# Three edits to a planned single-core kernel: who issues 32 stores, when four weight conversions run, and how far apart four weight combinations lie

## The chip, the cores and the metric

The program runs on 1 core of one Trainium2 chip. The metric is the device time of one execution in microseconds (us); less is better. Before the change it was 1371.14 us, the median of three runs (1365.4 to 1371.9).

The engines by their names in the rows: PE is the matrix engine (PEld its weight load), DVE the vector engine, ACT the scalar engine, POOL is GpSimd, and SP is the sync engine, which here only issues transfers (DMAs). A DMA stands in the instruction stream of the engine that issues it (SP, POOL or ACT); it can be issued only when all earlier instructions of that engine have been issued, and the data land some us later.

## The reference, cut to what matters

```python
# attention in chunks of 64 rows over q, k, v of shape (8, 8, 576, 64)
scores = matmul(q_c, k_c.T) / sqrt(64);  attn = softmax(scores);  out = matmul(attn, v_c)
x = out.transpose(0, 2, 1, 3).reshape(4608, 512)
# first MLP: 512 -> 2048 -> 512, softplus between
h = x @ w_in;  g = maximum(h, 0) + log1p(exp(-abs(h)));  x = g @ w_out
# second MLP: 512 -> 768 (three products, maximum of them) -> 512
y = maximum(maximum(x @ w1, x @ w2), x @ w3) @ w_out2
```

## The kernel before

**Numbers.** Products are wanted in near fp32. Every operand is kept as a high and a low part (`cut_up`: a copy to the rounded format gives the high part, a subtraction the low), and a product is three matmuls (high*high, high*low, low*high). The weights come as 64-bit floats; `conv` (lines 297 to 364) loads them as pairs of 32-bit words and builds the value on DVE in six steps (L332, L339, L346, L351, L357, L360), of which the last gives a rest that is added or cut up after it.

**Tiling.** The 4608 rows are nine blocks of 512. Each block has 16 steps of the first MLP (`mlp1`): an inner product (L805) into `ph`, softplus on ACT, `cut_up` into a buffer `g`, and an outer product (L825) into two accumulators `acc`.

**Stages in time.** (1) Blocks 0 to 2 (the blocks of `NP = 3`) go through `mlp1` step by step, in turns: block 0 steps 0 to 3, block 1 steps 0 to 7, block 0 steps 4 to 15, block 1 steps 8 to 15, block 2 steps 0 to 15. Meanwhile DVE converts the weights of the first MLP, and attention tiles for later blocks run (`attention`: loads of q, k and v, transposes on DVE, scores into `aps`, softmax, the probabilities `p` out to a DRAM buffer `pd` and back in another layout, values). (2) The other six blocks go in three pairs. A pair (A, B) has eight units (`UnitA`): seven products of half size (L1120, a Strassen scheme, products p1 to p7) give softplus inputs for two steps of both blocks. Softplus values of A (`h == 0`) are cut up into `g` at once and used by `mlp1_out` (L1419); those of B (`h == 1`) are written to DRAM (`gd`, line 1162, 16 in each of the first two pairs) and read again (line 1400) when A is done and B's 16 outer products follow. The third pair goes another way (`Sevens`): it keeps B's values on the chip and takes quarter products with combinations of the outer weights, which `combos` makes beforehand (16 DRAM tiles `wso`). (3) The second MLP (`Triple`) takes combinations of w1, w2 and w3 (`weights3`, DRAM tiles `w2c`), made from weights that `early` converted in stage 1 or 2 and stored (`w2d`, line 869; `wo2d`).

**What sets the order.** The kernel records operations with costs, inputs and due times, and `Plan.order` lays them out: a list scheduler with a modelled clock starts what is ready, the most urgent first, on an engine that is idle in its model, and gives out buffers. The result is a fixed order on every engine. So a change to a cost, an engine or a table shifts orders, buffers and waits of many operations near it. DMAs on SP and ACT take one of eight completion semaphores in turn (`DMAHW0` to `DMAHW7` in the rows of the built program; POOL's are `DMASW0` to `7`), and each waits, before it is issued, for the DMA that had the semaphore before it.

**Places touched.** `EARLIES` (line 978) says how many conversions `early` adds at each unit of each pair; `COMBOS` (line 986) after which of block B's outer products `combos` starts; line 1162 in `UnitA.soft` issues the store of a softplus value of B.

Of the kernel before, what the change touches and what calls it, by code (L numbers as in the profile page):

```python
# [183 lines left out]
def tile_kernel(ctx: ExitStack, tc: tile.TileContext, q, k, v, w_in, w_out, w1, w2, w3, wo2, out):  # L184
    nc = tc.nc
    B, H, S, D = q.shape
# [7 lines left out]
    NJ2 = DH2 // P  # L194
# [59 lines left out]
    gd = [[dram.tile([P, TB], F32, name=f"gd{i}_{j}") for j in range(NJ)] for i in range(3)]  # L254
# [36 lines left out]
    T0, STEP = 30.0, 6.0  # L291
# [674 lines left out]
    clock = [T1]  # L966
# [8 lines left out]
    EARLY = 8  # L975
    GATE = 7
    SPLITS = 6
    EARLIES = ((0, 0, 1, 1, 1, 1, 1, 1), (1,) * 8, (2, 2, 1, 1, 1, 1, 1, 1))
    GROUPS = (0, 1, 2, 3, 4, 6, 7)
    LATE_GROUPS = (1,)  # L980
    SPLIT = 1
# [1 line left out]
    GDLAT = 8.0  # L983
    SOON = 4
    SEVENS = (2,)
    COMBOS = (('out', 0, 1), ('out', 0, 4), ('out', 0, 7), ('out', 0, 10))
    LATER = (7, 0)
    SLACK = 0.0
    MORE = (3, 0), (5, 0), (5, 0)
# [113 lines left out]
    class UnitA:  # L1103
# [39 lines left out]
        def soft(u, src, z, fh):  # L1143
            c, (f, h) = u.c[fh], fh
            j = 2 * u.n + f
            if u.q in SEVENS:
                z2, at = raw_of(u.q, u.n, f, h), u.n % 2
                y = lambda: z2.t[:, at]
                in_line("y", op(
                    {"A": 0.62}, lambda e: nc.scalar.activation(y(), src(), AF.Softplus), r=[z], w=[(z2, at)], alloc=first_of(z2)  # L1150
                ))
                if h == 0:
                    g = second["a", NP + 2 * u.q, j] = Buf("g")
                    cut_up(g, y, [(z2, at)], alloc=[g])
                return
            in_line("y", op({"A": 0.62}, lambda e: nc.scalar.activation(c.t, src(), AF.Softplus), r=[z], w=[c], alloc=[] if z is c else [c]))
            if h == 0:
                g = second["a", NP + 2 * u.q, j] = Buf("g")
                cut_up(g, lambda: c.t, [c], alloc=[g])
            else:  # L1160
                store["g", u.q, j] = op(
                    {"S": 0.48}, lambda e: nc.sync.dma_start(out=gd[u.q][j], in_=c.t), r=[c], lat=6.0, move=1.1
                )

        def p1(u):
# [532 lines left out]

    def strassen():

        outs, earlies = [], 0
        tile_at = HP * NP + 2 * HP + 2

        def out(n=1):
# [14 lines left out]
        for q in range(pairs):  # L1719
            A, B = NP + 2 * q, NP + 2 * q + 1  # L1720
# [6 lines left out]
            for n, m in enumerate(ORDER[q]):  # L1727
                clock[0] = T0 + STEP * NJ * A + 17.7 * n
                new = UnitA(q, m)
                begin = new.p1()  # L1730
                mark["unit", q, n] = begin
                if ("unit", q, n) in COMBOS:
                    combos(COMBOS.index(("unit", q, n)), [begin], clock[0] + 30.0)
                if n == SEVENS_LOAD and sevens:
                    mark["sevens", q] = begin
                for _ in range(EARLIES[q][n]):
                    early(earlies, clock[0] + STEP * EARLY, [begin])
                    earlies += 1
                if q == pairs - 1:
                    mark[n] = begin  # L1740
                if not sevens:
                    out()
                if old:
                    old.p5()
                    old.p4()
                    if sevens:
                        out()
                    later(old.n, 1)
                new.p6()
                if old:  # L1750
                    old.p3()
                else:
                    out()
                new.p2()
                if not old:
                    out()
                new.p7()
                if n in GROUPS:
                    group()
                out()  # L1760
                later(m, 0)
                old = new
# [16 lines left out]
            for j in range(NJ - 2):  # L1779
                o = out()  # L1780
                if ("out", q, j) in COMBOS:
                    combos(COMBOS.index(("out", q, j)), [o], clock[0] + 30.0)
# [14 lines left out]
        for q in range(NB // 3):  # L1797
            u = Triple(q, banks, gate)
# [6 lines left out]
            for p in todo:  # L1805
# [3 lines left out]
                begin = u.product(*p, alloc=both if both[0].first is None else [])  # L1809
# [15 lines left out]
    for n, f in enumerate((1.0, -1.0)):  # L1825
        op(
            {"D": 0.2},
            lambda e, n=n, f=f: nc.vector.tensor_scalar(eye.t[:, n, :P], ident, f, None, ALU.mult),
# [8 lines left out]
    for j in range(NJ):  # L1837
# [4 lines left out]
        for t in range(HP, 2 * HP) if j == 1 else ():  # L1842
            attention_first(t, [line["load"]])
    tiles = 2 * HP
    for n, (b, j, first, last) in enumerate(steps):
        if n >= NJ and n % (NJ // HP) == 0:
            t = HP + n // (NJ // HP)
            t = 2 * HP + (n - NJ) // 2
            while tiles <= t + 1 and tiles < 22:
                attention(tiles, [first_loads[tiles if tiles < 2 * HP + 3 else NJ - 1]])  # L1850
                tiles += 1
        h = mlp1(b, j, first, last)
        if ("step", b, j) in COMBOS:
            combos(COMBOS.index(("step", b, j)), [h], T0 + STEP * (n + 4))
        if b == NP - 1 and j % 2 == 0:
            weightsa(j // 2, [before_last], lead)
        if (b, j) == (1, NJ // 2):
            lead = h
        before_last = h if j % 2 == 0 else before_last
# [38 lines left out]
```

## Time and profile before

| | |
|---|---|
| median of three runs | 1371.14 us (1365.4, 1371.14, 1371.9) |
| the profiled execution's own time | 1365.48 us |
| span of the profile, first to last instruction | 1363.6 us |
| PE busy | 1333.2 us, 98% of the span |
| DVE, ACT, POOL busy | 983.7, 545.0, 321.7 us |
| mean granted PE clock | 0.994 |

The span and 1.9 us around it make the execution's time. Busy time is a sum over stages; a stage is read by its own rows: in which stretch PE stands idle, on whom it waits there, and what that one waits for. "Idle before" names the engine or DMA whose end released an instruction; "issue" means that nothing in the profile explains the time (for an engine that issues DMAs, mostly a completion semaphore of an earlier DMA).

### The profile page before, as it was taken

The page shows a single profiled execution, that of the slowest core. Times are in us where ns is not written, and L with a number is a line of the kernel's source. Part 1 is how long each engine was busy: PE and PEld are TensorE (multiplying, and loading weights), DVE is VectorE, ACT ScalarE, POOL GpSimd, SP SyncE. Part 2 cuts the span into 40 slices and gives each one's busy share as a digit, 9 for nine tenths or more (in the row PEclk, how much of TensorE's full clock was granted, in tenths as well). Part 3 has the DMA queues.
Part 4 walks back from the last instruction along what each step waited for, and adds up shares of the span by engine and source line. Part 5 has one row for each costly group of instructions (what it writes and reads, how often), then busy time and mean ns, then how long its engine had stood idle before and what let it go on. Part 6 is the DMA issues. An engine that isn't in the chain of part 4 may idle for free.

```text
span 1363.6 us, 23089 instructions
## 1 busy us (share of the span) xinstructions
PE 1333.2 (98%) x8616; PEld 1094.0 (80%) x8616; DVE 983.7 (72%) x1527; ACT 545.0 (40%) x1199; POOL 321.7 (24%) x561
## 2 busy tenths in 40 slices
PE   5899999999999999999999999999999999999998
PEld 4788887888888887787788887888888888888887
DVE  8999965797576898657868898779714597145951
ACT  4544434464544645445535454432123222132211
POOL 2011555542233324323211122121111122011100
PEclk8999999999999999999999999999999999999999
DMA  8565567677689999978966789655644465344401
GB/s 254 159 201 154 134 181 201 189 273 228 169 257 258 267 302 301 280 252 297 366 209 237 259 311 338 234 192 193 219 162 144 155 231 206 141 148 154 139 25 68
DMA packets 218863, 289.38 MB, mean 212 GB/s; under 512 B 121601, under 2 KB 146625, under 8 KB 218753
## 3 DMA queue, kind: packets, MB, share of 16 engines
q0 software_dynamic: 53792, 178.26, 38.1%
q1 hardware_dynamic: 164144, 108.87, 26.9%
q8 instruction: 68, 1.11, 0.3%
q10 hardware_dynamic: 816, 0.79, 0.2%
q14 instruction: 43, 0.34, 0.1%
HBM read 196.61 MB, written 91.23 MB: 211 GB/s over the span
## 4 chain that ended last, share of the span: by engine, by line
PE 86%; DVE 5%; issue 4%; DMA 2%; POOL 1%; ACT 1%; SPq 0%; DVEq 0%; POOLq 0%; ACTq 0%
PE acc L1567 14%; PE both L1567 13%; PE acc L825 10%; PE ph L805 9%; PE ph L1120 8%; PE acc L1419 7%; PE one L1120 6%; PE both L1665 6%; PE acc L1665 5%; PE acc L1342 2%; PE ph L1342 2%; PE acc L1265 2%; DVE s L288 1%; PE aps L503 1%; POOL rv L468 1%
## 5 line engine op out<-in xcount | busy, mean ns | idle before, releaser
L288 DVE TENSOR_TENSOR s<-s,s 128x1024 f32<-128x1024 f32 (+3 forms) x222 | 213.8, 992 | 11.8 <-DMA x2d<-s 5.5
L1419 PE MATMUL acc<-g,s 128*128 128x512 f32 x768 | 184.5, 393 | 3.0 <-ACT tmp L281 2.2
L1419 PEld LDWEIGHTS acc<-g,s 128*128 128x128 f32 x768 | 142.6, 188 | 35.2 <-ACT tmp L281 3.1
L1120 PE MATMUL ph<-s,s 128*128 128x512 f32 x576 | 144.1, 389 | 1.4 <-DMA s<-wac 0.7
L805 PE MATMUL ph<-s,s 128*128 128x512 f32 x576 | 140.4, 394 | 0.0
L825 PE MATMUL acc<-g,s 128*128 128x512 f32 x576 | 139.8, 392 | 0.0
L1120 PEld LDWEIGHTS ph<-s,s 128*128 128x128 f32 x576 | 108.0, 188 | 24.6 <-DMA s<-wac 1.2
L805 PEld LDWEIGHTS ph<-s,s 128*128 128x128 f32 x576 | 108.3, 189 | 23.1
L825 PEld LDWEIGHTS acc<-g,s 128*128 128x128 f32 x576 | 107.3, 188 | 22.6
L281 ACT CAST s<-s 128x512 fp32r<-128x512 f32 (+1 forms) x106 | 86.3, 831 | 93.4 <-DVE s L1598 31.2
L1567 PE MATMUL acc<-s,s 128*128 128x512 f32 x452 | 120.3, 389 | 0.0
L1550 POOL DMA_DIRECT2D s<-w2c x105 | 56.0, 533 | 266.2 <-PE both L1567 87.5
L281 ACT CAST g<-s 128x1024 fp32r<-128x1024 f32 (+1 forms) x64 | 58.7, 919 | 144.6 <-PE both L1567 37.3
L1567 PE MATMUL acc<-g,s 128*128 128x512 f32 x400 | 110.0, 389 | 0.0
L1120 PE MATMUL one<-s,s 128*128 128x512 f32 x432 | 106.4, 390 | 0.9 <-ACT p L562 0.9
L1567 PE MATMUL both<-s,s 128*128 128x512 f32 x400 | 106.3, 389 | 0.0
L288 DVE TENSOR_TENSOR g<-tmp,g 128x512 fp32r<-128x512 f32 x104 | 70.6, 680 | 44.3 <-ACT g L281 44.2
L1567 PE MATMUL both<-g,s 128*128 128x512 f32 x368 | 100.1, 389 | 0.0
L1567 PEld LDWEIGHTS acc<-s,s 128*128 128x128 f32 x452 | 84.9, 188 | 17.6
L1120 PEld LDWEIGHTS one<-s,s 128*128 128x128 f32 x432 | 80.9, 188 | 18.5 <-ACT p L562 1.8
L468 POOL DMA_DIRECT2D rv<-in_v_dram x103 | 63.5, 620 | 104.5 <-issue 55.3
L1567 PEld LDWEIGHTS both<-s,s 128*128 128x128 f32 x400 | 75.1, 188 | 15.6
(158 smaller groups left out, 2159.5 us busy)
## 6 DMA issues: line engine op xcount, KB each, us to landing
s<-w2c POOLq DMA_DIRECT2D x105, 512.0 KB, 4.5
s<-wac POOLq DMA_DIRECT2D x66, 512.0 KB, 6.5
w2c<-s POOLq DMA_DIRECT2D x45, 512.0 KB, 5.2
wac<-s POOLq DMA_DIRECT2D x24, 512.0 KB, 5.1
s<-in_moe_w_dram POOLq DMA_DIRECT2D x18, 512.0 KB, 5.6
s<-x2d POOLq DMA_DIRECT2D x18, 512.0 KB, 5.8
s<-in_moe_w_in_dram SPq DMA_DIRECT2D x16, 512.0 KB, 6.2
s<-in_moe_w_out_dram SPq DMA_DIRECT2D x16, 512.0 KB, 5.7
```

The costliest lines, as they stand in the source:

```text
L281: nc.scalar.copy(dst(), src())
L288: return op({"D": 0.69 * n}, lambda e: nc.vector.tensor_tensor(dst(), a(), b(), f), r=r, w=w, **kw)
L468: dma(out=dst().rearrange("p (c e d) -> p c e d", e=2, d=D)[half * CH:(half + 1) * CH, lo:lo + mine, h, :], in_=v[b, t % HP * 2 + h].rearr ...
L805: nc.tensor.matmul(ph.t, w[:, wi, kk * P:(kk + 1) * P], x[kk].t[:, xi], start=(kk == 0 and wi == 0 and xi == 0), stop=(kk == KD - 1 and wi ...
L825: nc.tensor.matmul(acc[m // 2].t[:, m % 2], w[:, wi, m * P:(m + 1) * P], g.t[:, gi, :], start=(first and wi == 0 and gi == 0), stop=(last ...
L1120: nc.tensor.matmul(dst(), ws.t[:, wi, col + kk * P:col + (kk + 1) * P], x[kk].t[:, xi], start=(first and kk == 0 and wi == 0 and xi == 0), ...
L1265: nc.tensor.matmul(u.acc[f].t[:, m], w.t[:, wi, m * P:(m + 1) * P], g.t[:, gi, :], start=(first and wi == 0 and gi == 0), stop=(last and w ...
L1342: nc.tensor.matmul(dst(m), lhs(wi, nn, m), (GH, GL)[gi].t[:, nn], start=(fresh and nn == 0 and wi == 0 and gi == 0), stop=(nn == 1 and wi ...
L1419: nc.tensor.matmul(acc[half].t[:, m % 2], w.t[:, wi, m * P:(m + 1) * P], g.t[:, gi, :], start=(first and wi == 0 and gi == 0), stop=(last ...
L1550: lambda e, k=k, z=z: nc.gpsimd.dma_start(out=z.t.bitcast(F32), in_=w2c[s][late + k]),
L1567: nc.tensor.matmul(bank.view()[:, f], ws(wi, slice(f * HT + kk * P, f * HT + (kk + 1) * P)), (XH, XL)[xi].t[:, kk], start=(first and kk == ...
L1665: nc.tensor.matmul(banks[t // 2].view()[:, t % 2], (GH, GL)[gi].t[:, f, t * P:(t + 1) * P], wo2_of[j].t[:, wi], start=(j == 0 and wi == 0 ...
```

## The change

`BEFORE` is new: four conversions for the second MLP are recorded right after steps 9, 11, 13 and 15 of block 1 of the first MLP. They are the first four of the list; so the units of the first pair take six less two, none at its last two units, and the second pair takes none at its first two units. The total stays 24. `COMBOS` starts the four combinations after outer products 1, 5, 9 and 13 of block B of the first pair; before, after 1, 4, 7 and 10. The stores to `gd` are planned on ACT, at a cost of 0.5 in the plan, and issued there.

```diff
-    EARLIES = ((0, 0, 1, 1, 1, 1, 1, 1), (1,) * 8, (2, 2, 1, 1, 1, 1, 1, 1))
+    EARLIES = ((0, 0, 1, 1, 1, 1, 0, 0), (0, 0, 1, 1, 1, 1, 1, 1), (2, 2, 1, 1, 1, 1, 1, 1))
+    BEFORE = ((1, 9), (1, 11), (1, 13), (1, 15))
...
-    COMBOS = (('out', 0, 1), ('out', 0, 4), ('out', 0, 7), ('out', 0, 10))
+    COMBOS = (('out', 0, 1), ('out', 0, 5), ('out', 0, 9), ('out', 0, 13))
...
                 store["g", u.q, j] = op(
-                    {"S": 0.48}, lambda e: nc.sync.dma_start(out=gd[u.q][j], in_=c.t), r=[c], lat=6.0, move=1.1
+                    {"A": 0.5}, lambda e: nc.scalar.dma_start(out=gd[u.q][j], in_=c.t), r=[c], lat=6.0, move=1.1
                 )
...
-        outs, earlies = [], 0
+        outs = []
...
                 for _ in range(EARLIES[q][n]):
-                    early(earlies, clock[0] + STEP * EARLY, [begin])
-                    earlies += 1
+                    early(next(earlies), clock[0] + STEP * EARLY, [begin])
...
+    earlies = iter(range(4 * NJ2 + 6))
     for n, (b, j, first, last) in enumerate(steps):
...
         h = mlp1(b, j, first, last)
+        if (b, j) in BEFORE:
+            early(next(earlies), T0 + STEP * (n + EARLY), [h])
```

The order on PE stays as it was but for one attention product, which moves behind one outer product. On the other engines it moves at many places. Three of them follow.

**ACT, first pair, where the values of steps 2 and 3 of block B are stored.** `tmp<-tmp` and `tmp<-ph` (L1156, in the new file L1157) are softplus; `CAST g<-tmp` gives the high part for an outer product; `COPY tmp<-ph` empties the bank into which PE's next product goes. Before:

```order
L1156 ACTIVATE tmp_79<-tmp_79 128x512 [waits DVE_49]
L1156 ACTIVATE tmp_83<-ph_93 128x512 [waits PE_49,Activation_49]
L281 CAST g_76<-tmp_83 128x512 [waits Activation_49]
L281 COPY tmp_85<-ph_92 128x512 [waits DMAHW1_49,PE_49]
L1156 ACTIVATE tmp_84<-tmp_84 128x512 [waits DVE_49]
L1156 ACTIVATE tmp_80<-tmp_80 128x512 [waits DVE_49]
L281 COPY tmp_86<-ph_92 128x512 [waits PE_49]
L281 CAST g_77<-tmp_80 128x512 [waits Activation_49]
```

Now:

```order
L1157 ACTIVATE tmp_84<-tmp_84 128x512 [waits DVE_49]
L1157 ACTIVATE tmp_85<-ph_93 128x512 [waits DMAHW0_49,PE_49]
L1163 DMA gd_3_110<-tmp_84 128x512 [waits DMAHW2_49,Activation_49]
L281 CAST g_76<-tmp_85 128x512 [waits Activation_49]
L281 COPY tmp_86<-ph_92 128x512 [waits DMAHW3_49,PE_49]
L1157 ACTIVATE tmp_82<-tmp_82 128x512 [waits DVE_49]
L1163 DMA gd_2_109<-tmp_82 128x512 [waits DMAHW0_49,Activation_49]
L1157 ACTIVATE tmp_83<-tmp_83 128x512 [waits DVE_49]
L281 COPY tmp_80<-ph_92 128x512 [waits DMAHW1_49,PE_49]
L281 CAST g_77<-tmp_83 128x512 [waits Activation_49]
```

Two stores stand in ACT's stream, one ahead of each copy out of `ph`; each waits for a completion semaphore that it shares with SP's DMAs, and for the softplus before it.

**DVE, second half of block 1 of the first MLP.** `mx` and `p` are an attention tile's softmax, L751 turns `p` for its way through `pd`, and L698 and L699 turn the next tile's q and k. Before:

```order
L288 TENSOR_TENSOR s_113_2790<-aps_94,s_113_2790 128x512
L698 STREAM_TRANSPOSE s_114_2811<-rq_74 128x512
L699 STREAM_TRANSPOSE s_114_2811<-tmp_78 128x512
L590 TENSOR_SCALAR mx_70<-mx_70 128x8
L591 RECIPROCAL mx_70<-mx_70 128x8
L288 TENSOR_TENSOR p_89<-p_89,mx_70 128x512
L751 STREAM_TRANSPOSE s_115_2853<-p_89 128x512
```

Now:

```order
L332 TENSOR_SCALAR tmp_86<-s_110_2638 128x512
L698 STREAM_TRANSPOSE s_114_2811<-rq_74 128x512
L339 TENSOR_SCALAR tmp_86<-tmp_86 128x512
L699 STREAM_TRANSPOSE s_114_2811<-tmp_78 128x512
L346 TENSOR_SCALAR tmp_86<-tmp_86 128x512
L351 SCALAR_TENSOR_TENSOR tmp_86<-s_110_2638,tmp_86 128x512
L590 TENSOR_SCALAR mx_70<-mx_70 128x8
L357 TENSOR_SCALAR tmp_79<-tmp_86 128x512
L591 RECIPROCAL mx_70<-mx_70 128x8
L360 SCALAR_TENSOR_TENSOR tmp_79<-s_110_2638,tmp_79 128x512
L288 TENSOR_TENSOR p_89<-p_89,mx_70 128x512
L288 TENSOR_TENSOR tmp_86<-tmp_86,tmp_79 128x512
```

A conversion's seven instructions lie between those of the softmax; its first, L332, waits for a weight load that POOL issues.

**POOL, from block B of the first pair into the second pair.** `wso` are the stores of the combinations, `wac` and `wae` loads of Strassen weights, `rv` an attention tile's values, and L318 the load that a conversion starts from. Before:

```order
L468 DMA rv_88<-in_v_dram 64x4x64 x2
L468 DMA rv_88<-in_v_dram 64x3x64 x2
L468 DMA rv_88<-in_v_dram 64x64 x2
L1233 DMA wso_3_231<-s_268_6096 128x1024
L318 DMA s_269_6135<-in_moe_w_dram 128x4x256
L1233 DMA wso_3_235<-s_270_6146 128x1024
L1045 DMA s_272_6183<-wac_2_163 128x1024
L1233 DMA wso_3_239<-s_271_6171 128x1024
L1233 DMA wso_3_243<-s_273_6187 128x1024
L1045 DMA s_275_6219<-wac_1_162 128x1024
L1045 DMA s_276_6257<-wae_180 128x1024
```

Now:

```order
L468 DMA rv_88<-in_v_dram 64x4x64 x2
L468 DMA rv_88<-in_v_dram 64x3x64 x2
L468 DMA rv_88<-in_v_dram 64x64 x2
L1234 DMA wso_3_231<-s_268_6094 128x1024
L1234 DMA wso_3_235<-s_270_6132 128x1024
L1234 DMA wso_3_239<-s_271_6160 128x1024
L1234 DMA wso_3_243<-s_272_6167 128x1024
L1046 DMA s_274_6199<-wac_2_163 128x1024
L1046 DMA s_275_6227<-wac_1_162 128x1024
L1046 DMA s_276_6264<-wae_180 128x1024
```

The load for a conversion is gone from here (as is one a little ahead of it), and the last four `wso` stores stand together, ahead of the Strassen loads.

## Rows read from the trace of the kernel before

**Rows 1.** The page: span and busy us by engine.

```profile
span 1363.6 us, 23089 instructions
PE 1333.2 (98%) x8616; PEld 1094.0 (80%) x8616; DVE 983.7 (72%) x1527; ACT 545.0 (40%) x1199; POOL 321.7 (24%) x561
```

**Rows 2.** Busy us by stretch: PE, PEld, DVE, ACT, POOL; clock, DMA share, GB/s.

```profile
0.00:40.00 40.00, 24.94 (x655) 19.82 (x656) 33.38 (x77) 17.48 (x50) 8.44 (x19) 0.84 0.85 251
...
200.00:345.00 145.00, 143.89 (x1222) 117.62 (x1216) 108.60 (x225) 75.30 (x267) 62.90 (x109) 1.00 0.74 223
345.00:440.00 95.00, 95.00 (x712) 77.96 (x711) 56.83 (x110) 45.17 (x135) 29.57 (x49) 1.00 0.81 236
440.00:560.00 120.00, 117.64 (x803) 94.61 (x802) 103.67 (x196) 63.81 (x183) 39.41 (x66) 1.00 0.96 291
...
600.00:720.00 120.00, 117.06 (x628) 95.31 (x628) 85.71 (x151) 59.47 (x118) 30.87 (x53) 1.00 0.80 285
```

**Rows 3.** PE's waits, 440 to 560 us: us, times, longest.

```profile
PE one L1120 <- ACT p L562: 0.9, 2, 0.6
PE ph L1120 <- DMA s<-wac: 0.7, 1, 0.7
PE acc L1419 <- DVE g L288: 0.4, 1, 0.4
PE acc L1419 <- ACT tmp L281: 0.3, 1, 0.3
```

**Rows 4.** PE's waits, 600 to 720 us.

```profile
PE acc L1419 <- ACT tmp L281: 2.0, 1, 2.0
PE ph L1120 <- ACT tmp L281: 0.7, 1, 0.7
PE acc L1419 <- DVE g L288: 0.3, 1, 0.3
```

**Rows 5.** PE's waits, 195 to 345 us.

```profile
PE aps L503 <- DMA s<-pd: 1.1, 2, 0.6
```

**Rows 6.** POOL in order of time, 536 to 546 us: start, us, idle before.

```profile
537.65 0.63 POOL L468 DMA_DIRECT2D rv<-in_v_dram  x1 [3.31 <-issue]
540.84 0.62 POOL L468 DMA_DIRECT2D rv<-in_v_dram  x1 [2.56 <-issue]
...
544.62 0.80 POOL L318 DMA_DIRECT2D s<-in_moe_w_dram  x1 [0.23 <-DMA s<-pd]
```

**Rows 7.** DVE in order of time, 546 to 556 us.

```profile
550.56 0.43 DVE L332 TENSOR_SCALAR tmp<-s 128x512 int32<-128x512 int32 x1 [3.85 <-DMA s<-in_moe_w_dram]
```

**Rows 8.** DVE groups of a conversion: count, busy us, mean ns, idle before.

```profile
L351 DVE SCALAR_TENSOR_TENSOR tmp<-s,tmp 128x512 int32<-128x512 int32 x56 | 38.1, 681 | 0.5
...
L332 DVE TENSOR_SCALAR tmp<-s 128x512 int32<-128x512 int32 x56 | 23.8, 425 | 10.1 <-DMA s<-in_moe_w_dram 6.5 <-DMA s<-in_moe_w_in_dram 3.6
...
L288 DVE TENSOR_TENSOR tmp<-tmp,tmp 128x512 f32<-128x512 f32 x18 | 12.2, 678 | 0.2
```

**Rows 9.** SP's own waits: us in total, times, longest.

```profile
SPq L1162 <- ACT tmp L1156: 41.7, 17, 5.4
...
SPq L443 <- DMA rq<-in_q_dram: 8.1, 7, 2.4
```

**Rows 10.** The stores to gd: ns of the issue, min, median, max.

```profile
L1162 SPq DMA_DIRECT2D gd<-tmp x32: 319/344/1407, 349.7 to 649.0; - x32
```

**Rows 11.** ACT in order of time, its only DMA issues.

```profile
0.77 1.55 ACTq L429 DMA_DIRECT2D s<-in_q_dram  x3
```

**Rows 12.** ACT in order of time, 396 to 413 us: a copy out of ph.

```profile
400.01 0.58 ACT L281 COPY tmp<-ph 128x512 f32<-128x512 f32 x1
```

**Rows 13.** PE in order of time: the next product into that bank.

```profile
402.38 1.29 PE L1120 MATMUL ph<-s,s 128*128 128x512 f32 x5
```

**Rows 14.** POOL in order of time, 620 to 650 us.

```profile
639.12 0.62 POOL L468 DMA_DIRECT2D rv<-in_v_dram  x1 [2.98 <-PE one L1120]
639.73 0.56 POOL L926 DMA_DIRECT2D w2c<-s  x1
```

**Rows 15.** ACT in order of time, 634 to 650 us.

```profile
643.54 0.62 ACT L281 CAST s<-s 128x512 fp32r<-128x512 f32 x1 [3.27 <-DMA w2c<-s]
```

**Rows 16.** Transfers: issues, KB each, median us to landing.

```profile
s<-in_moe_w_dram POOLq DMA_DIRECT2D x18, 512.0 KB, 5.6
...
w2d<-tmp SPq DMA_DIRECT2D x18, 256.0 KB, 4.7
```

## The prediction

> **What bounds the kernel now.** I read the page first, then the busy times by stretch, then PE's waits in each stretch that the change reaches, and last, for the longest of these waits, the engine that was waited for. PE is busy for 1333.2 of 1363.6 us [rows 1], so 30.4 us are all that any reordering could give back. By stretch [rows 2], 15.1 us of it lie in the first 40 us, ahead of everything that the change touches. In the stretches that it does touch, PE is idle for 1.1 us (200 to 345), 0.0 (345 to 440), 2.4 (440 to 560) and 2.9 (600 to 720): 6.4 us together, 0.5% of the time. The reader is to see that the 40 idle per cent of ACT and DVE's 28 per cent say little here: PE's own matmuls set the time, and the question is which few waits go and which come.
>
> The waits have three sources. From 440 to 560 us the DMA engines are busy for 96% [rows 2]; PE waits there for a softmax on ACT (0.9), for a Strassen weight load (0.7), and for parts of `g` and emptied banks (0.4 and 0.3) [rows 3]. One chain can be followed: POOL's loads of attention values stand 3.31 and 2.56 us apart without an engine to blame, so the weight load of a conversion behind them is issued only at 544.62 [rows 6]; DVE stands in front of that conversion for 3.85 us [rows 7], and the softmax and the loads behind it come late. From 600 to 720 us the 2.0 us wait [rows 4] has another source: POOL's store of a combination `w2c` is queued behind a load that waited 2.98 us for PE [rows 14], ACT waits 3.27 us for that store before a cast [rows 15], and the copies that empty the accumulators stand behind the cast. From 200 to 345 us PE waits twice for `pd`, an attention tile's probabilities on their way through DRAM [rows 5].
>
> **The change part by part.** The sum is made against the profiled execution's own time, 1365.48 us (its span and 1.9 us around it), not against the median of 1371.14, which lies 5.7 us higher with nothing in this profile to show where.
>
> *The conversions.* One costs DVE four plain steps at 0.425, two at 0.681 and one addition at 0.678, together 3.74 us [rows 8], and the DMA engines a 512 KB load and a 256 KB store [rows 16]. Four of them leave 424 to 525 us and come to about 200 to 260. Where they leave, 15.0 us of DVE work go, and 3 MB, which at the stretch's 291 GB/s [rows 2] are some 10 us of all DMA engines. The load of [rows 6] stays where it is; two loads ahead of it go, and the four last `wso` stores move together. So the chain gets shorter, not cut. Of the 2.4 us I take the 0.7 of the weight load and half of the other 1.7: 1.5 us gained. The bounds are 0 and 2.4.
>
> Where they come, DVE has 108.6 of 145 us busy and POOL 62.9 [rows 2], so the engines have room; but a conversion is placed in the middle of a softmax, and its first step waits for a load that POOL issues among attention's small loads. In the trace such waits are 6.5 us in all [rows 8], 3.85 in the longest, which leaves 2.65 for the others. A hold of DVE delays `p`, `pd` and then a product on PE that already waited 1.1 us [rows 5]. The price per us held is seen once: 0.6 us on PE, the longest wait for the softmax [rows 3], behind the 3.85 of [rows 7], 0.16 per us. Four new holds of 1.6 us (a quarter of the 6.5) make 1.0 us lost, which I take. Bounds: 1.1 gained, if the shifted products no longer meet `pd` early, and 4 times 3.85 = 15.4 lost, if PE lost all that DVE is held.
>
> *The combinations.* Each starts some outer products later: the last after the 14th of block B and no longer after the 11th. The same instructions, spread over a longer stretch; their DVE work now overlaps the second pair's first two units, which in exchange lose a conversion each. They are read only in the third pair, after 720 us. I take 0 and count their share in the 1.5 us above; bounds are the 0.7 us of waits for `g` and banks in [rows 3], either way.
>
> *The waits from 600 to 720.* The POOL queue and the ACT casts at 640 us stand as before, except that a store comes between the copies of the accumulators. I take 0; bounds: 2.9 us gained, 1 us lost (a store's issue at 0.3 to 0.5 us, twice).
>
> *The stores on ACT.* SP issues 32 of them in 0.344 us each by the median [rows 10], 11.0 us; ACT's own three issues took 1.55 us, 0.52 each [rows 11], 16.5 us. So ACT gets 11 to 17 us more in a stretch in which it is idle for 49.8 us (345 to 440) and 56.2 (440 to 560) [rows 2]. Idle time is not all that counts: behind a store, ACT's next instructions are the cast for `g` and the copy that empties `ph`. One copy ended at 400.58 [rows 12], and PE wrote that bank at 402.38 [rows 13]: 1.8 us to spare. An issue of 0.52 us fits in it, and so does the longest that SP shows, 1.41. Cost taken: 0. Without that cover it would be up to 16.5 us.
>
> What hangs on the added wait: each store waits for a completion semaphore that one of SP's DMAs, eight places earlier in the planned order, had before it. Queued behind are the softplus, the casts and the copies of the unit; PE waits for those. SP's waits of that kind are short, 8.1 us in 7 waits for the q loads, the longest 2.4 [rows 9], and eight DMAs earlier is mostly several us earlier. I take 0.
>
> The Trainium skill (the page "DMA: Bandwidth & Descriptors", section "Anatomy of one DMA — SWDGE (gpsimd) path") says that a DMA engine never waits for a semaphore: the wait happens on the issuing sequencer, before dispatch. By that rule ACT's sequencer stands for the whole of such a wait, which is the second rival below. The trace agrees as far as it goes, since SP shows just such waits; no run here shows one on ACT yet.
>
> *SP's relief.* SP loses 32 issues, and 41.7 us in which it stood in front of a store until ACT had the softplus ready [rows 9]. Its loads can go earlier. But from 345 to 720 us PE waits for none of SP's transfers [rows 3, 4]. I take 0 to 1 us of gain, so 0.
>
> Sum: -1.5 + 1.0 + 0 + 0 = -0.5 us, or 1365.0 us in terms of the profiled execution. The four executions shown (three runs and the profile) lie at 1365.4, 1365.5, 1371.1 and 1371.9, and a median of a few new ones can fall at either level; so the sum is put on their median, 1368.3, which gives **1367.8 us**. With either level, 1365.0 or 1370.6, it is the same verdict: no change.
>
> **The rivals.** *First, the relief is larger.* If 3 MB less in a stretch with 96% busy DMA engines and 15 us less on DVE end every wait from 200 to 720 us, 6.4 us go: 1359.1 us for the profiled execution. And if the 5.7 us by which two runs are longer are these same waits, grown with the transfers, they go too, and the median falls to about 1362. For it: the DMA share, and that the one chain that could be followed in that stretch leads back to a transfer [rows 6, 7]. Against it: the 2.0 us wait hangs on POOL's queue at 640 us, which is not changed.
>
> *Second, slower: the stores hold ACT.* Place: the 16 units of the first two pairs, at the copy out of `ph`. Price: with a wait of 2.4 us, SP's longest of that kind [rows 9], and an issue of 0.52, a store holds ACT for 2.9 us; less the 1.8 us that there is to spare, PE loses 1.1 us in each of 16 units, 18 us: 1383 us. It decides from 1.3 us of semaphore wait on; below that it costs nothing. For it: the wait is new on ACT, and SP runs late at times (an issue of 1.41 us). Against it: on SP these waits average 1.2 us, and ACT reaches the store only when the softplus is done, which was when SP had already waited for it in 17 of 32 cases.
>
> *Third, the gain is eaten in the second half of block 1.* If PE loses all that DVE is held, four holds of 1.6 us cost 6.4 us; less the 1.5 us gained it is 1370.4 us in terms of the profiled execution. For it: no spare time at `pd` [rows 5]. Against it: only 0.16 us per us held was lost where it can be seen.
>
> **How the numbers follow.** Half a per cent, 6.9 us, is about what a measurement of this kernel can tell from no change. Chances: forecast 0.51, first rival 0.25, second 0.10, third 0.14. Faster by over 0.5% means below 1364.3 us: the first rival mostly (0.20), and 0.05 from a forecast at the lower level with a little more gain: 0.25. Slower means above 1378.0 us: the second rival, 0.10. The rest, 0.65, is no change. The range leaves out the second rival and the far end of the first: 1361 us (1365.5 less 4.5 of the 6.4 us) to 1375 us (the longest run, 1371.9, with 3 us more of the third rival).
>
> **What would show it.** Right: in the changed kernel's profile PE's idle time from 440 to 560 us is near 1 us, with the wait for `wac` gone; the 2 us wait near 640 us stands; 1 to 2 us more of PE waits for `pd` or `aps` lie between 200 and 260 us, with DVE's L332 waiting for a weight load ahead of them; ACT's stores take 0.3 to 0.6 us each, and no copy out of `ph` is waited for. Wrong: PE waits for ACT's copies in many units of 345 to 690 us with ACT standing in front of L1163 (second rival); PE idle for less than 2 us in all from 200 to 720 us (first); PE waits of several us between 200 and 345 us (third).

## The result, and the profile after

The changed kernel takes 1382.14 us (median of 6 runs), the kernel before, beside it on the same chip, 1369.61 (6 runs): a ratio of 1.0099, 95% interval [1.0084, 1.0114], some 13 us slower. Predicted were 1367.8 us with a range of 1361 to 1375.

The page of the changed kernel, for [rows 1]:

```profile
span 1379.5 us, 23106 instructions
PE 1336.0 (97%) x8616; PEld 1094.7 (79%) x8616; DVE 986.4 (72%) x1534; ACT 541.7 (39%) x1192; POOL 318.6 (23%) x558
```

The span is 15.9 us longer. PE is busy 2.8 us longer with the same 8616 matmuls, and idle 13.1 us longer (43.5 against 30.4). The busy times by stretch, for [rows 2], say where; behind 345 us the windows are put later by the 12 to 17 us that the kernel is late there, so that they hold about the same work:

```profile
0.00:40.00 40.00, 23.05 (x658) 18.15 (x659) 34.15 (x79) 17.61 (x50) 7.99 (x19) 0.87 0.87 256
...
200.00:345.00 145.00, 134.22 (x1094) 109.07 (x1094) 105.70 (x222) 67.58 (x239) 60.67 (x102) 0.96 0.67 202
345.00:457.00 112.00, 110.75 (x836) 90.17 (x836) 70.18 (x135) 54.17 (x171) 32.51 (x55) 1.00 0.87 253
457.00:577.00 120.00, 117.50 (x806) 95.21 (x805) 95.25 (x179) 60.71 (x171) 37.75 (x65) 1.00 0.88 269
...
617.00:737.00 120.00, 116.64 (x624) 94.58 (x623) 85.77 (x152) 58.44 (x116) 30.90 (x53) 1.00 0.79 280
```

From 200 to 345 us PE is idle for 10.8 us; it was 1.1. That is 9.7 of the 13.1. Another 1.2 lie between 345 and 457, 1.9 in the first 40 us, which the change does not reach, and nearly nothing elsewhere. A window in us cuts off the work that comes late. Between the same two matmuls (at 195 and 360 us before the change) the kernel before needs 164.9 us and the changed one 181.2: 16.3 us more, of which 10.9 are idle and 5.4 longer busy time. All engines do less in that stretch than before, DVE and POOL too: nobody is overloaded, everybody waits. PE's waits from 195 to 345 us, for [rows 5]:

```profile
PE aps L503 <- ACT p L562: 5.0, 1, 5.0
PE acc L825 <- DVE g L288: 3.5, 1, 3.5
PE aps L503 <- DMA s<-pd: 2.2, 1, 2.2
```

Two are attention products whose tile comes late, one is an outer product. One step back, DVE in order of time at the first step of the conversions that moved (start, us, instruction, idle before it and who ended that):

```profile
229.88 0.43 DVE L332 TENSOR_SCALAR tmp<-s 128x512 int32<-128x512 int32 x1 [10.65 <-DMA s<-in_moe_w_dram]
...
242.53 0.43 DVE L332 TENSOR_SCALAR tmp<-s 128x512 int32<-128x512 int32 x1 [5.62 <-DMA s<-in_moe_w_dram]
...
263.63 0.43 DVE L332 TENSOR_SCALAR tmp<-s 128x512 int32<-128x512 int32 x1 [5.05 <-issue]
```

The four loads landed at 207.94, 229.85, 242.50 and 263.55 us by their completion events, so the last of these holds, too, ended with a load, though the view has no name for it. DVE stood 21 us in front of three weight loads, between 219 and 264 us. PE's waits of 5.0 and 2.2 us come behind the first two of these holds. The wait of 3.5 us does not: it comes behind a hold of 8.81 us at an attention transpose, which ended when a store of POOL's (`wac`, issued only at 289.15, behind a row of k loads) had landed at 294.93:

```profile
294.95 0.71 DVE L698 STREAM_TRANSPOSE s<-tmp 128x512 f32<-128x512 f32 x1 [8.81 <-DMA wac<-s]
```

And one step back again, POOL, which issues these loads (L318) among attention's small loads of k and v:

```profile
225.91 0.78 POOL L318 DMA_DIRECT2D s<-in_moe_w_dram  x1 [3.09 <-issue]
226.68 0.61 POOL L443 DMA_DIRECT2D tmp<-in_k_dram  x1
230.16 1.90 POOL L443 DMA_DIRECT2D tmp<-in_k_dram  x3 [2.87 <-issue]
...
236.34 0.79 POOL L318 DMA_DIRECT2D s<-in_moe_w_dram  x1
238.25 1.17 POOL L468 DMA_DIRECT2D tmp<-in_v_dram  x2 [1.12 <-issue]
242.83 0.64 POOL L468 DMA_DIRECT2D tmp<-in_v_dram  x1 [3.42 <-issue]
...
258.55 0.78 POOL L318 DMA_DIRECT2D s<-in_moe_w_dram  x1 [1.25 <-issue]
259.32 0.60 POOL L443 DMA_DIRECT2D tmp<-in_k_dram  x1
263.85 1.85 POOL L443 DMA_DIRECT2D tmp<-in_k_dram  x3 [3.94 <-issue]
```

This is the row to learn to read. Behind each of these loads POOL issues one or two transfers, stands for 2.9 to 3.9 us, and goes on at 230.16, 242.83 and 263.85: 0.3 us after the load has landed, each time (and at 208.25 after the first, landed at 207.94). The profile has only "issue" for what it waits for, but the landings tell more. All 24 stops of over 0.2 us that the view calls "issue" between 195 and 270 us end 0.31 to 0.35 us after the landing of a transfer that POOL itself had issued two to four places before (two only where a 512 KB load is the one that landed or the one that waits). It is not the completion semaphore: the transfer eight places before had landed at least 4.3 us earlier each time. So POOL has only a few transfers under way, and one that lands late holds up all that it has still to issue. Such stops are not new (from 195 to 345 us in front of k loads 30.4 us in 30 of them before the change, 24.4 us in 24 now); new is that a 512 KB load is among the few. The longest hold of DVE, too, is in the main POOL's: it began at 219.23, the load was issued at 225.91 and took 3.94 us.

The rest of the loss is PE's clock. Around the idle times of 4.97 and 3.48 us the granted clock falls, and matmuls take longer: of the 181.2 us above, 10.2 are at 1.2 GHz, of the 164.9 before none. PE in order of time, then two short windows:

```profile
234.38 1.22 PE L503 MATMUL aps<-s,rv 64*64 64x64 f32 x31 [4.97 <-ACT p L562]
...
297.90 4.37 PE L825 MATMUL acc<-g,s 128*128 128x512 f32 x11 [3.48 <-DVE g L288]
```

```profile
297.00:303.00 6.00, 5.10 (x63) 3.96 (x67) 5.93 (x13) 2.68 (x6) 0.55 (x2) 0.72 0.45 160
230.00:240.00 10.00, 5.62 (x73) 4.73 (x74) 6.77 (x15) 5.29 (x21) 6.75 (x11) 0.68 0.48 133
```

At 297.90 eleven matmuls take 4.37 us, where twelve of the same product take 2.88 at full clock: 0.40 us each against 0.24. The clock of 0.72 and 0.68 in these windows is a mixture of the two levels, 1.2 and 2.4 GHz, behind idle times of 3.48 and 4.97 us.

Where the conversions left, PE's waits from 457 to 577 us, for [rows 3], and the one long wait of [rows 4]:

```profile
PE one L1121 <- DVE tmp L288: 1.1, 1, 1.1
PE ph L1121 <- DMA s<-wac: 0.8, 1, 0.8
PE one L1121 <- ACT p L562: 0.7, 1, 0.7
```

```profile
PE acc L1420 <- ACT tmp L281: 1.9, 1, 1.9
```

2.5 us idle against 2.4, although DVE has 8 us less to do there: no gain that the profile shows. The stores on ACT cost next to nothing: ns of the issue as in [rows 10], and of the semaphore waits in front of them, which ACT passed in 17 ns each. It is SP's loads that now stand behind them (last line; it was 3.8 us before):

```profile
L1163 ACTq DMA_DIRECT2D gd<-tmp x32: 326/326/373, 367.4 to 663.8; - x32
L1163 ACTq EVENT_SEMAPHORE  x31: 17/17/17, 367.4 to 663.3; - x31
```

```profile
SPq L443 <- DMA gd<-tmp: 26.8, 10, 7.8
```

### The profile page after: what moved, and what is told of

Read it like the earlier page. It is cut to its first block, busy times and chain, and to the rows that moved or that the text cites. A ratio compares the mean times of both kernels' runs of the same rounds, so it can differ in the third digit from the quotient of the medians.

```text
span 1379.5 us, 23106 instructions
## 1 busy us (share of the span) xinstructions
PE 1336.0 (97%) x8616; PEld 1094.7 (79%) x8616; DVE 986.4 (72%) x1534; ACT 541.7 (39%) x1192; POOL 318.6 (23%) x558
## 4 chain that ended last, share of the span: by engine, by line
PE 81%; DVE 6%; issue 6%; POOL 4%; DMA 2%; ACT 1%; SPq 0%; DVEq 0%; POOLq 0%; ACTq 0%
PE acc L1568 14%; PE both L1568 13%; PE acc L1420 11%; PE ph L1121 8%; PE one L1121 6%; PE acc L825 6%; PE both L1666 6%; PE ph L805 5%; PE acc L1666 5%; PE acc L1343 2%; POOL tmp L443 2%; PE ph L1343 2%; PE acc L1266 2%; DVE s L288 1%; DVE tmp L288 1%
## 5 line engine op out<-in xcount | busy, mean ns | idle before, releaser
L1420 PEld LDWEIGHTS acc<-g,s 128*128 128x128 f32 x768 | 142.8, 188 | 34.0 <-ACT tmp L281 2.3
L825 PEld LDWEIGHTS acc<-g,s 128*128 128x128 f32 x576 | 109.8, 192 | 27.5 <-DVE g L288 3.9
L281 ACT CAST s<-s 128x1024 fp32r<-128x1024 f32 (+1 forms) x99 | 81.9, 845 | 90.9 <-DVE s L1599 31.2
L1568 PEld LDWEIGHTS acc<-g,s 128*128 128x128 f32 x400 | 75.1, 188 | 15.6
```

Source lines behind the costliest of these rows:

```text
L281: nc.scalar.copy(dst(), src())
L825: nc.tensor.matmul(acc[m // 2].t[:, m % 2], w[:, wi, m * P:(m + 1) * P], g.t[:, gi, :], start=(first and wi == 0 and gi == 0), stop=(last ...
L1420: nc.tensor.matmul(acc[half].t[:, m % 2], w.t[:, wi, m * P:(m + 1) * P], g.t[:, gi, :], start=(first and wi == 0 and gi == 0), stop=(last ...
L1568: nc.tensor.matmul(bank.view()[:, f], ws(wi, slice(f * HT + kk * P, f * HT + (kk + 1) * P)), (XH, XL)[xi].t[:, kk], start=(first and kk == ...
```

## The experiments

In the tables "idle" is PE's idle time in the window from 200 to 345 us, in the one execution that was profiled. The ratio is to the kernel before, on the same chip.

### Which part of the change

Three kernels: the changed one without the move, the kernel before with nothing but the move, and with nothing but the stores on ACT.

```diff
# e1: changed kernel
-    BEFORE = ((1, 9), (1, 11), (1, 13), (1, 15))
+    BEFORE = ()          # and EARLIES as before the change
# e2: kernel before, with the changed EARLIES and BEFORE alone
# e3: kernel before, with this alone
-    {"S": 0.48}, lambda e: nc.sync.dma_start(out=gd[u.q][j], in_=c.t)
+    {"A": 0.5}, lambda e: nc.scalar.dma_start(out=gd[u.q][j], in_=c.t)
```

> The changed kernel with its conversions put back to where they were (24 in the units, none in block 1 of the first MLP); the stores on ACT and the wider combinations stay. Theory (vector engine held in block 1 by late weight loads): the 13 us are gone, 1364 to 1371 us, ratio to before 0.996 to 1.001, and PE is idle for 2 us at most between 200 and 345 us. Rival (the stores hold ACT): still about 1382 us, ratio 1.01.

> The kernel before with the four conversions moved into block 1, and nothing else. Theory (vector engine held by late weight loads): 1380 to 1386 us, ratio 1.008 to 1.012; DVE stands for 10 us in front of one of the moved conversions, and PE loses 10 us or more between 200 and 345 us. Rival (stores on ACT): 1366 to 1371 us, ratio 1.0.

> The kernel before with the 32 stores issued on ACT, and nothing else. Theory: no change that can be told, 1364 to 1373 us, ratio 0.996 to 1.003, since ACT issues a store in 0.33 us beside its waits. Rival (the stores hold ACT): 1378 us or more.

| | us | ratio | idle |
|---|---|---|---|
| e1, all but the move | 1368.32 | 1.0002 [0.9985, 1.0019] | 0.8 |
| e2, the move alone | 1382.71 | 1.0107 [1.0074, 1.0139] | 8.2 |
| e3, the stores alone | 1368.96 | 1.0005 [0.9988, 1.0023] | 0.9 |

The move is the whole loss. (In e2 the window holds less idle time than the 10 us that were expected; 2.8 us more lie in the 15 us behind it.) The stores on ACT alone, and together with the wider combinations, make no difference that can be told, within some 3 us; the rival by which ACT's stores hold the units is out. Both profiles have a wait of PE that is new, 4.6 us (e1) and 3.9 us (e3) near 533 us, for an attention product; the times do not show it, and it was not followed.

### DVE's hold, or what is behind it

First the holds alone were aimed at: the plan was told that the four loads take 22 us to land instead of 9, so that it puts DVE's steps 105 to 163 matmuls behind the load (17 to 92 in the changed kernel).

```diff
-    op({by: 0.5}, load, w=[raw], alloc=[free, raw], after=after, lat=9.0 if by == "G" else 2.0, ...)
+    op({by: 0.5}, load, w=[raw], alloc=[free, raw], after=after, lat=lat if by == "G" else 2.0, ...)  # 22.0 for the four
```

> The changed kernel, with the planned latency of the four moved loads raised from 9 to 22, so that DVE's steps of these conversions stand later in its order (105 to 163 matmuls behind the place of the load, in place of 17 to 92); the loads, the 15 us of DVE work, the bytes and the stage stay the same. Theory (DVE held by a load that POOL issues late): DVE stands for less than 2 us in front of each conversion and most of the loss goes, 1366 to 1373 us. Rival (the work itself, or its transfers, is too much for the stage): 1379 to 1385 us, with PE's waits in the same stretch.

1381.3 us, 1.0091 [1.0064, 1.0117]: not what was expected. DVE no longer waits at L332, but it does for attention's own k:

```profile
230.97 0.71 DVE L699 STREAM_TRANSPOSE s<-tmp 128x512 f32<-128x512 f32 x1 [4.12 <-DMA tmp<-in_k_dram]
231.61 0.39 DVE L332 TENSOR_SCALAR tmp<-s 128x512 int32<-128x512 int32 x1
...
258.94 0.71 DVE L699 STREAM_TRANSPOSE s<-tmp 128x512 f32<-128x512 f32 x1 [4.31 <-DMA tmp<-in_k_dram]
```

Idle is 4.2 us here and 2.1 in the 15 us behind the window, about half of the changed kernel's 10.8 and 1.2; but the new plan also made the late wait of [rows 4] 6.4 us long in place of 2.0. So the theory lost its first form (DVE is held) and the time of a re-planned kernel turned out to be a poor witness. From here on, most runs keep the changed kernel's order, instruction by instruction, and edit only what an instruction does.

### The load, its bytes and its queue, in one order

```diff
         def load(e):
+            if moved: return                                        # e5: no load
+            if moved: <load of 64 words per partition>; return      # e9: 32 KB
+            if moved: <load of 256 words per partition>; return     # e13: 128 KB
-            start = (nc.gpsimd if e == "G" else nc.sync).dma_start
+            start = (nc.gpsimd if e == "G" and not moved else nc.sync).dma_start              # e7: SP
+            start = (nc.scalar if moved else nc.gpsimd if e == "G" else nc.sync).dma_start    # e10, e14: ACT
-        hw = lambda: raw.t[:, :, 1]
+        hw = lambda: old()[:, :, 1] if moved else raw.t[:, :, 1]    # e5, e6, e9, e13, e14: DVE reads a resident weight
```

> The changed kernel, same instruction order, with the four loads of the conversions that moved into block 1 left out: their VectorE steps run at the same places on a weight that is long on the chip (so these four parts of the second MLP's weights are not the right values). Theory (POOL's in-order queue is late because of the four 512 KB loads, and VectorE's work itself costs next to nothing): the loss of about 14 us between 222 and 450 us goes, the gain of 1.8 us behind 447 us stays, so 1365 to 1369 us, TensorE's waits in 195-360 us below 2 us. Rival (the VectorE steps themselves, some 3 us a conversion, are too much in that stretch, or the moved order as such is bad): 1377 to 1382 us, TensorE still waiting some 8 us there.

> The changed kernel, same order, with the four moved loads kept on POOL, but the VectorE steps of these conversions read a weight that is long on the chip, so that VectorE waits for no such load (the four parts are not the right values). Theory (POOL's queue, whatever VectorE waits for): attention's k and v loads stand behind the four loads as before, so 1375 to 1382 us, VectorE's holds now at attention's own loads. Rival (VectorE's holds of 10.6 and 5.6 us at the conversions' first step are the cause, POOL's queue alone costs little): 1366 to 1370 us.

> The changed kernel, same order, with the four moved loads issued by SyncE in place of POOL. Theory (it is POOL's queue, with attention's k loads in it): POOL is on time again; SyncE's queue holds attention's q loads and the turns through DRAM, so some of the loss may come back there: 1367 to 1374 us. Rival (bytes: 2 MB more on the DMA engines in that stretch, whoever issues them): 1378 to 1384 us.

> The changed kernel, same order, with each of the four moved loads cut from 512 KB to 32 KB (128 partitions x 64 words; VectorE's steps read a weight that is long on the chip and wait for no load, as in the run without them; the four parts are not the right values). POOL still issues an instruction for each. Theory A (what the load costs the queue is the time that its 512 KB take to move, 4 to 7 us each, which the transfers behind it wait out): 1366 to 1369 us, POOL on time. Theory B (each load costs the queue a turn of a few us whatever its size): as with the 512 KB loads that nobody waits for, 1376 to 1380 us.

> The changed kernel, same order, with the four moved loads issued by ScalarE in place of POOL (0.33 us of ScalarE for each, in a stretch in which it is busy 17 of 40 us, and no attention load in its queue). Theory (POOL's queue is the cause): POOL stays as it is without the loads, so the loss goes and the gain of the later stretch stays, 1366 to 1369 us, at or below the kernel before. Rival (the load's wait for its buffer, or its 2 MB beside attention's transfers, costs as much in any queue that the block uses): 1372 to 1378 us, as with SyncE or worse, with TensorE waiting for ScalarE or for attention's transfers.

> As the run with the four moved loads cut to 32 KB and read by nobody, but with 128 KB each (128 partitions x 256 words; the four parts of the weights are not the right values). Theory (bytes: what is lost grows with the bytes in front of attention's small transfers; 10.5 us lay between 32 KB and 512 KB, a fifth of that way is 128 KB): 1369 to 1372 us. Rival (any load of more than a few KB costs POOL a turn, or the loss is a matter of a threshold that is passed early): 1374 to 1379 us.

> The changed kernel, same order, with the four 512 KB loads issued by ScalarE and read by nobody (VectorE's steps read a weight that is long on the chip; the four parts are not the right values). Theory (the bytes on the shared DMA engines, whoever issues them): attention's small transfers on POOL still land late behind each load, 1373 to 1377 us. Rival (the loss with ScalarE's loads came from VectorE's wait for them, POOL's queue being the only other cost): 1366 to 1369 us.

| each of the four loads | us | ratio | idle | PE late | POOL late |
|---|---|---|---|---|---|
| none (e5) | 1367.44 | 0.9974 [0.9954, 0.9993] | 0.0 | 0 | 0 |
| 32 KB on POOL, unread (e9) | 1368.22 | 0.9982 [0.9965, 1.0000] | 0.6 | 0.1 | 1.0 |
| 128 KB on POOL, unread (e13) | 1366.28 | 0.9987 [0.9970, 1.0004] | 2.2 | 2.5 | 3.5 |
| 512 KB on ACT, unread (e14) | 1372.96 | 1.0037 [1.0012, 1.0062] | 5.7 | 10.8 | 12.4 |
| 512 KB on POOL, unread (e6) | 1378.75 | 1.0061 [1.0040, 1.0081] | 7.9 | 14.1 | 14.0 |
| 512 KB on SP, read (e7) | 1373.11 | 1.0026 [1.0007, 1.0045] | 4.3 | 6.1 | 6.9 |
| 512 KB on ACT, read (e10) | 1376.78 | 1.0056 [1.0035, 1.0078] | 6.1 | 10.0 | 11.4 |
| 512 KB on POOL, read (changed) | 1382.14 | 1.0099 [1.0084, 1.0114] | 10.8 | 16.8 | 16.4 |

As the order is the same in all of them, the same instruction can be sought in each trace. "PE late" is by how many us more than in e5 PE needs from the matmul that stands at 195 us in e5 to the one at 360; "POOL late" is the same for POOL, from its transfer at 196 us to the last of its k loads, at 275. Both follow one profiled execution, as idle does; those of e9 and e13 are the fastest of their ten runs, that of e14 (1377.84 us) one of the slower.

The idle times are read from the windows, here those of e5, e13 and e6:

```profile
200.00:345.00 145.00, 145.00 (x1281) 118.41 (x1280) 121.28 (x250) 76.26 (x266) 63.56 (x109) 1.00 0.72 217
```

```profile
200.00:345.00 145.00, 142.77 (x1210) 116.41 (x1209) 119.54 (x250) 75.68 (x268) 62.86 (x107) 1.00 0.72 217
```

```profile
200.00:345.00 145.00, 137.08 (x1110) 110.89 (x1108) 108.12 (x226) 68.28 (x240) 61.12 (x102) 0.98 0.68 207
```

What follows, one at a time.

DVE's work costs nothing. In e5 DVE does all the steps of the four conversions in that stretch, 121.28 us of busy time, and PE is not idle at all there (0.7 us in the 15 us behind).

The size of the load costs, and nearly in proportion. On POOL, with DVE waiting for none of them, idle grows 0.6, 2.2, 7.9 us with 32, 128 and 512 KB; the line through the first two would give 8.6 at the third. Bytes and pieces are not separated by this: 512 KB are 512 pieces of 1 KB, 128 KB are 128 of them, 32 KB are 128 of 256 bytes. A POOL instruction as such, or a turn of its queue, is cheap: e9 has them all. The times are less sharp than the idle: e13's is a little below the 1369 to 1372 that was expected, and its interval overlaps e9's and holds 1, so that 128 KB show no loss in time; but both lie clear of e6. In e6 POOL stands behind the loads as in the changed kernel:

```profile
257.64 0.78 POOL L318 DMA_DIRECT2D s<-in_moe_w_dram  x1 [2.08 <-issue]
258.79 0.60 POOL L444 DMA_DIRECT2D tmp<-in_k_dram  x1 [0.36 <-issue]
263.80 1.74 POOL L444 DMA_DIRECT2D tmp<-in_k_dram  x3 [4.41 <-issue]
```

The queue matters less than I had thought. I expected ACT's loads to be nearly free, 1366 to 1369 us, and got 1376.78: that form of the theory (POOL's queue is the cause) falls, and its rival is right in size; with nobody reading the loads (e14) 1372.96 us remain, just under the 1373 to 1377 that the bytes were to cost. POOL falls behind in all of these runs, by about as much as PE (last columns), and it stands still although the load is not in its queue. ACT's fourth load, then POOL behind it, in e10:

```profile
240.23 0.40 ACTq L318 DMA_DIRECT2D s<-in_moe_w_dram  x1
```

```profile
240.70 1.78 POOL L443 DMA_DIRECT2D tmp<-in_k_dram  x3 [3.13 <-issue]
248.44 1.83 POOL L443 DMA_DIRECT2D tmp<-in_k_dram  x3 [5.97 <-issue]
```

The load is on its way from 240.23 to 248.63. The three k transfers of 32 KB that POOL issues meanwhile land between 248.14 and 249.15, 7 us after their issue, where the median of this run is 2.8 us and the same three take 3.0 to 4.4 us in e5; and POOL goes on at 248.44, 0.3 us after the first of its own three has landed. Three loads of 256 KB that SP had issued from 239.46 to 240.55 were under way there as well, so not all of the 7 us need be the 512 KB's. Behind ACT's load of 218.11, landed at 223.02, the next four of POOL's land between 223.56 and 224.71. So attention's small transfers, issued a few at a time, land with the 512 KB that are under way, whoever issued these. The Trainium skill (the page "DMA: Bandwidth & Descriptors", section "Queues, rings and completion order") says that a DMA engine takes turns between queues packet by packet; by that, 32 KB from another queue should get through well ahead of 512 KB. The trace does not bear this out at this place: by its packets, none of the three moved before 245.04 us, when 402 of the load's 512 KB had moved, and they came out together.

What DVE's wait for the loads adds is the step from e6 to the changed kernel, 1.0061 to 1.0099, 2.9 us more idle (PE late: 2.7). On ACT the same step, e14 to e10, does not show: 0.4 us more idle, PE 0.7 us less late, and the intervals overlap. SP's loads cost least of the three, near the upper end of the 1367 to 1374 us that were expected; their interval overlaps ACT's, and why they cost less, if they do, was not settled.

### Fewer, and elsewhere

```diff
# e8: two of the four in block 1, the other two in the first pair's last two units
+    EARLIES = ((0, 0, 1, 1, 1, 1, 1, 1), (0, 0, 1, 1, 1, 1, 1, 1), (2, 2, 1, 1, 1, 1, 1, 1))
+    BEFORE = ((1, 13), (1, 15))
# e11: none in block 1, four in the first pair's first two units
+    EARLIES = ((2, 2, 1, 1, 1, 1, 0, 0), (0, 0, 1, 1, 1, 1, 1, 1), (2, 2, 1, 1, 1, 1, 1, 1))
# e12: two there
+    EARLIES = ((1, 1, 1, 1, 1, 1, 1, 1), (0, 0, 1, 1, 1, 1, 1, 1), (2, 2, 1, 1, 1, 1, 1, 1))
```

> The changed kernel with two conversions moved instead of four (steps 13 and 15 of block 1; the other two stay in block 2's first units' places, as before the change). Theory (each load that POOL gets in that stretch makes it later, about 3.5 us for each): half the loss, 1374 to 1377 us. Rival (it is the first loads, at steps 9 and 11, whose first use stands only 17 and 28 matmuls behind the load, or all that are moved are needed to fill the queue): 1368 to 1371 us.

> The changed kernel with the four conversions moved to another place: not into block 1, but into the first two units behind the blocks (some 345 to 380 us; two each), where POOL is busy 10 to 15 of 40 us and the transfers of attention's tiles are fewer. Theory (a 512 KB load costs where a chain of small attention transfers has to get through behind it, and little elsewhere; the stretch that the conversions leave gains 2 to 3 us): 1365 to 1369 us, a ratio of 0.996 to 1.000. Rival (a load costs PE some 3.5 us wherever it is put early, as TensorE waits for attention there too): 1373 to 1382 us.

> As the run with four at the units' start, but with two conversions moved (one each in the first two units behind the blocks, the other two staying in the last two units of that row). Theory: about half the gain, 1367 to 1369.5 us, a ratio of 0.998 to 1.000. Rival (cost of 3.5 us for each load): 1372 to 1376 us.

(In e8 the other two conversions stand in the first pair's last two units, as the diff has it.) e8: 1378.76 us, 1.0067 [1.0047, 1.0086]; e11: 1372.01, 1.0030 [1.0011, 1.0050]; e12: 1385.08, 1.0115 [1.0091, 1.0139]. All three times are above what the theory gave, and e12, with two loads, is slower than e11 with four.

In the stretch itself the theory holds: idle is 4.3 us with two loads (e8), and 0.8 and 0.2 with none there (e11, e12); and from 360 to 440 us, where e11 and e12 put them, PE is not idle in either. Much of what these kernels lose lies at the wait of [rows 4], which the new plans made longer: 6.5 us in e8, 4.6 in e11, 6.8 in e12, in place of 2.0. e11 has another new one, 3.5 us at 445.68, for an attention tile's softmax. In e12 the cause is the one seen there before ([rows 15], 3.27 us), only later: ACT, then PE.

```profile
649.82 1.66 ACT L281 CAST s<-s 128x512 fp32r<-128x512 f32 x3 [4.47 <-DMA w2c<-s]
```

```profile
655.68 31.60 PE L1420 MATMUL acc<-g,s 128*128 128x512 f32 x132 [6.77 <-ACT tmp L281]
```

e12 has another of 7.2 us at 882 us. So moving conversions re-plans stores and combinations hundreds of us later, and that can cost as much as what was aimed at. Why the plan comes out so in one case and not in the other was not followed further. No complete kernel was found that beats the one before: the two with a ratio clearly below 1 or at its edge leave loads out (e5) or cut them (e9).

## Why the prediction was wrong

The failed step is the term of the conversions that arrive: "Four new holds of 1.6 us (a quarter of the 6.5) make 1.0 us lost, which I take." It was mis-sized: between the same two matmuls PE lost 16.3 us, 10.9 idle and 5.4 at the lower clock, a little over the upper bound of 15.4 that the text gave and set aside; e2, with the move alone, is slower by about as much (1.0107, some 14.6 us). Three things went into it.

- *The hold.* 1.6 us was a mean over waits of the kernel before, where a load is issued among other traffic; at the new place the holds are 10.65, 5.62 and 5.05 us.
- *The price per us held.* 0.16 came from one softmax wait behind one hold. Here PE's waits of 5.0 and 2.2 us come behind some 21 us held, about 0.34; where attention already ran without slack [rows 5], the hold arrives at PE. PE's third wait, 3.5 us, comes behind a hold that the term did not have, 8.8 us for a store late in POOL's queue; nor did it have the clock.
- *What was left out.* The term priced DVE's hold alone. The load itself, as 512 KB in front of attention's small transfers, was counted nowhere: "the engines have room" was said of DVE's and POOL's busy time. With the hold gone and the load kept, 1.0061 remains (e6); with the load gone and DVE's work kept, 0.9974 (e5).

The third rival had the right place and sign, with the same too short holds. It took the hold of DVE for the mechanism; that is the smaller part.

*The conversions that leave* (1.5 us gained): not shown. PE's idle there is 2.5 us against 2.4, and the `wac` wait, which was to go, is 0.8 us. e5 gives 3.6 us in time by its ratio, but it also leaves out 2 MB, and its profile has no shorter span; the gain stays open between 0 and that. The first rival, in which these waits go, did not happen.

*The combinations* and *the stores on ACT* (0 each): as measured, 1.0002 for both together and 1.0005 for the stores alone. An issue on ACT takes 0.326 us; the semaphore waits in front of it, from 1.3 us on the condition of the second rival, took 0.017 us. PE waits for a copy out of `ph` twice in those units, 0.2 and 0.7 us, and the 0.7 stood there before [rows 4]. That SP's relief is worth nothing holds too; the wait has only changed sides.

*The wait near 640 us* stood, 1.9 against 2.0, as predicted for this change. That it moves to 4.6 to 6.8 us under other plans had not been thought of.

Two readings were wrong without weight in the sum. ACT is idle for 60% of the span, not 40. And SP's longest wait for an earlier transfer in front of a store to `gd` was 3.5 us; the 2.4 that the second rival was priced with is from its q loads.

## What to carry to other kernels

When a transfer is moved, price its bytes at the new place before the work of the engine that uses it: ask which small transfers on the critical path will be issued while it is under way, and take its time to landing, once for each load and whoever issues it, as a price from above. (Here the four landing times add up to 22.3 us on POOL, 27.6 on ACT and 21.6 on SP; PE came 16.8, 10.0 and 6.1 us late.) A stretch in which the other engines have time to spare can still be full, if its path runs through a chain of short transfers issued a few at a time. And where a planner sets the order, test a cause in one fixed order, since a re-planned kernel changes places far from the edit.

## What had not been expected of the hardware

- POOL went on 0.31 to 0.33 us after a 512 KB load had landed, four times out of four, with one to three small issues in between. The wait has no name in the profile. It is for POOL's own earlier transfers: in e5, without these loads, all 28 such stops between 195 and 270 us also end 0.31 to 0.33 us after the landing of a transfer, there three to five places before. What sets how many it can have under way (their number, bytes or pieces) was not tried.
- It stood in the same way when the load was ACT's (5.97 us), since its own 32 KB transfers landed 7 us after their issue, with the 512 KB of the other queue.
- An idle time of 3.5 us on PE was followed by a stretch at a granted clock of 0.72, in which eleven matmuls took 4.37 us in place of 2.64: 1.7 us on top of the wait.
